# A plain first layer in block 1, x of block 2 transposed on PE, and another order of m-tiles in a chunk-attention and MLP kernel

## Chip, cores, metric

The kernel runs on one core of a Trainium2 chip. The metric is the device time of one execution in microseconds (us). A ratio is the mean time of one kernel's fast runs over that of the other's fast runs of the same rounds, so not quite the ratio of the medians quoted beside it. "Trace" below is one profiled execution; its span is 1.5 to 2 us less than the time measured for it. PE is the TensorE, DVE the VectorE, ACT the ScalarE, POOL the GpSimd; PSUM is the memory, in banks, that PE writes its products to. In the 40 slices of a profile's page, slices are counted from 0.

## The reference, cut

```python
def _attn_ref(q, k, v):                      # each (8, 8, 576, 64)
    # nine chunks of 64 per sequence; softmax attention inside each chunk
    scores = scale * np.matmul(q_c, k_c.transpose(0, 1, 2, 4, 3))
    ...
    return out.reshape(B, H, S, D)

def _moe_ref(x, w_in, w_out, beta):          # x (4608, 512), w_in (512, 2048), w_out (2048, 512)
    h = x @ w_in
    g = h * (1.0 / (1.0 + np.exp(-beta * h)))
    return (g @ w_out).astype(np.float32)
```

x is the attention's output, tokens by heads times head size. Inputs and output are float32; the kernel computes in float16 with float32 sums.

## The kernel before

The 4608 tokens are done in nine blocks of 512. Each block needs x transposed (`xt`, four tiles of 128 tokens), then L1 (16 m-tiles of 128 hidden features, Silu on ACT) and L2. From block 1 on, half of L1 (m-tiles 0 to 7) and all of L2 use seven half-size products in place of eight, after Strassen and Winograd; they need sums of x (`emit_xs`), of the weights (`emit_sw` for L1, `emit_tw` for L2) and of the hidden values (`emit_sum`). While block j is in its layers, scores (`emit_sc`) and value products (`emit_pv`) of block j+1 are slipped between its products. In the profile: L131 the DVE transposes of q and k (`T`), L159 a product of scores, L187 a value product, L202 and L204 its normalisation, L224 the copy of an x tile transposed on PE, L245 a plain m-tile, L278 to L281 `emit_xs`, L298 a product of a unit, L306, L319 and L333 the unit's snapshots and sums on DVE, L309 its Silu, L370 `emit_tw`, L356 to L362 `emit_sum`, L398 a product of L2. Of the tiles, `sc` holds scores, `hps` a plain m-tile, `wA` and `wX` a unit's products, and `oA` to `oD` those of L2, all in PSUM.

A transposed tile on PE, and one unit, which makes four m-tiles:

```python
    def emit_xp(i):
        xf = x16_t.pop(i)
        j, t0 = i // 4, (i % 4) * 128
        xps = ps_s.tile([128, KDM, 128], FP16, tag=f"sc{i % 2}", name="xps")
        for kk in range(KDM):
            nc.tensor.transpose(
                out=xps[:, kk, :], in_=xf[:, kk * 128:(kk + 1) * 128], identity=ident
            )
        nc.scalar.copy(out=xt_t[j][:, :, t0:t0 + 128], in_=xps)

    def unit(j, q, spacers):
        x = xt_t[j]
        ts = xs_t[j]
        up_, dn_ = slice(0, HT), slice(HT, BLK)
        b11, b21, b22 = x[:, 0:2, up_], x[:, 2:4, up_], x[:, 2:4, dn_]
        swr = [t.rearrange("p k (m i r) -> p k m r i", r=2, i=128) for t in sw]
        a11, a12, a22 = w_r[0][:, 0::2], w_r[0][:, 1::2], w_r[1][:, 1::2]
        bank = {"A": ps_s.tile([128, 2, HT], FP32, tag=f"sc{q}", name="wA")}
        xx = ps_x.tile([128, 2, 2, HT], FP32, tag="x", name="wX")
        bank["B"], bank["C"] = xx[:, 0], xx[:, 1]
        sb = {}

        def prod(b, a, rhs, first):
            for i in range(2):
                for kk in range(2):
                    nc.tensor.matmul(
                        out=bank[b][:, i, :], lhsT=a[:, kk, q, i, :], rhs=rhs[:, kk, :],
                        start=(first and i == 0 and kk == 0), stop=(kk == 1),
                        skip_group_check=True,
                    )

        def snap(nm, b):
            sb[nm] = u_p.tile([128, 2, HT], FP32, tag=nm, name=nm)
            nc.vector.tensor_copy(out=sb[nm], in_=bank[b])

        def silu(m, cols, src):
            nc.scalar.activation(
                out=gt_t[j][:, m, cols], in_=src, func=ACTF.Silu,
                scale=beta2[:, m % 2, m // 2:m // 2 + 1],
            )

        m1, m2 = 2 * q, 4 + 2 * q
        c1 = c_p.tile([128, 2, BLK], FP32, tag="c1", name="c1")
        prod("A", a11, b11, True)
        snap("u1", "A")
        prod("B", a12, b21, True)
        nc.vector.tensor_tensor(out=c1[:, :, up_], in0=bank["B"], in1=sb["u1"], op=ALU.add)
        spacers[0]()
        prod("A", swr[1], ts[1], False)
        snap("u2", "A")
        prod("C", swr[0], ts[0], True)
        snap("w1", "C")
        spacers[1]()
        prod("A", swr[2], ts[2], False)
        snap("u3", "A")
        sb["t"] = u_p.tile([128, 2, HT], FP32, tag="t", name="t")
        nc.gpsimd.tensor_tensor(out=sb["t"], in0=sb["u3"], in1=sb["w1"], op=ALU.add)
        spacers[2]()
        prod("A", a22, ts[3], False)
        prod("C", swr[3], b22, False)
        nc.vector.tensor_tensor(out=c1[:, :, dn_], in0=bank["C"], in1=sb["u2"], op=ALU.add)
        for i in range(2):
            silu(m2 + i, up_, bank["A"][:, i])
        for i in range(2):
            silu(m1 + i, slice(0, BLK), c1[:, i])
        for i in range(2):
            silu(m2 + i, dn_, sb["t"][:, i])
```

The first layer, plain and with units; a hook is other work slipped in ahead of an m-tile:

```python
    def L1_plain(j, hooks, nh):
        for m in range(nh):
            emit_h(j, m, 0, HT)
            hooks.get(-1 - m, lambda: None)()
        for m in range(nh):
            emit_h(j, m, HT, BLK)
            emit_g(j, m)
        for m in range(nh, KFF):
            emit_m(j, m)

    def L1(j, hooks={}, first=None):
        gt_t[j] = gt_p.tile([128, KFF, BLK], FP16, tag="gt", name="gt")

        def sp(m):
            def f():
                hooks.get(m, lambda: None)()
                emit_m(j, m)
            return f

        if first:
            first()
        unit(j, 0, [sp(8), sp(9), sp(10)])
        sp(11)()
        unit(j, 1, [sp(12), sp(13), sp(14)])
        for p in (0, 2):
            emit_sum(j, 3, p)
        sp(15)()
        for p in (0, 2, 1, 3):
            fill.extend([lambda w=w, p=p: emit_sum(j, w, p) for w in (1, 2)])
        hooks.get(KFF, lambda: None)()
```

The end of block 0's stretch on DVE, and the loop over blocks:

```python
        emit_sw()
        scale_w_out(0)
        scale_w_out(1)
        T1 = T_items(1)
        T1[0]()
        T1[1]()
        scale_w_out(2)
        T1[2]()
        T1[3]()
        scale_w_out(3)
        load_v(2)
        load_qk(3)
        emit_tw(1)
        emit_tw(2)
        ...
        emit_xp(7)
        emit_xs(1)
        emit_tw(4)
        emit_tw(3)
        for j in range(1, NB):
            na = j + 1
            if j == 1:
                order = (2, 2, 2, 2)
            elif j == 2:
                order = (3, 3, 4, 4)
            else:
                order = (j + 2,) * 4
            hooks = {m: (lambda b=b: T(b)) for m, b in zip((10, 11, 14, 15), order)}
            late = j <= 2
            if late:
                hooks[KFF] = lambda: [table(ACTF.Exp), emit_sc(2 * na)]
            L1(j, hooks)

            def pv(n):
                if na < NB:
                    emit_pv(4 * na + n)

            def sc(n):
                if na + 1 < NB and j > 1:
                    emit_sc(2 * na + 2 + n)

            if j > 1 and j + 3 < B or j == 1:
                load_qk(j + 3)
            mm, cB, cD, cC = steps_L2(j, last=(j == NB - 1))
            mm[0]()
            emit_sum(j, 3, 1)
            emit_sum(j, 3, 3)
            if not late:
                pv(0)
            dve(4)
            mm[1]()
            if late:
                pv(0)
                emit_sc(2 * na + 1)
            else:
                pv(1)
            cB()
            dve(2)
            mm[2]()
            pv(1 if late else 2)
            dve(2)
            mm[3]()
            pv(2 if late else 3)
            if not late:
                table(ACTF.Exp)
                sc(0)
            for p in range(4):
                emit_sum(j, 4, p)
            if j == 2:
                T(4, 2)
            mm[4]()
            cD()
            if late:
                pv(3)
                sc(0)
            mm[5]()
            if j < NB - 1:
                cC()
            if not late:
                sc(1)
            if j == 1:
                T(3, 2)
            if na < NB:
                emit_xs(na)
            mm[6]()
            if late:
                sc(1)
            table(ACTF.Silu)
            if j + 2 < B:
                load_v(j + 2)
```

The softmax here doesn't subtract the row's maximum and nothing guards it: scores larger than these inputs give would overflow.

## Time and profile before

| | before |
|---|---|
| time, median (runs) | 310.49 us (4 runs, 309.58 to 311.74) |
| span of the trace | 309.8 us |
| PE, DVE, ACT, POOL busy | 89, 73, 54, 33% |
| mean granted PE clock | 0.977 |
| block 0's L2 ends, block 1's L1 starts | 55.5 us |
| blocks 1, 2, 3, 4 (start of L1 to start of the next) | 36.5, 36.3, 33.3, 31.4 us |
| blocks 5, 6, 7, 8 | 29.5, 29.1, 28.2, 29.9 us |

PE's idle time is not spread out. Blocks 6 and 7 run at the pace that PE allows; blocks 1 and 2 are seven to eight microseconds longer for the same layers. A change that is to pay has to make the first blocks look like the last.

### The profile page before, as it was taken

To read this page: it belongs to the slowest core of one execution; us is meant where nothing else is said; L and a number is where in the kernel's file an instruction comes from. 1 tells how busy PE (TensorE), PEld (TensorE's weight loads), DVE (VectorE), ACT (ScalarE), POOL (GpSimd) and SP (SyncE) were. 2 spreads that over 40 slices of the span, in tenths; PEclk is the share of its full clock that TensorE was granted. 3 is DMA by queue.
4 is the path that set the end of the run, shared out by engine and by line. 5 is a ranking of instruction groups with operands and counts; after the bars stand their busy time and mean duration, and the time that the engine had idled before them with its cause. 6 is when DMAs were issued, how large, how long until landed. Compare 5 with 4: busy or idle time off the path is not lost.

```text
span 309.8 us, 8218 instructions
## 1 busy us (share of the span) xinstructions
PE 276.0 (89%) x3520; PEld 190.4 (61%) x3520; DVE 225.1 (73%) x415; ACT 168.8 (54%) x291; POOL 101.7 (33%) x110
## 2 busy tenths in 40 slices
PE   2689997498996999799989997999999999999995
PEld 0364443255883668555866586658866876676584
DVE  2682466768797879788868886889765976687584
ACT  1258333437713793557437733773577457536852
POOL 8632260014215161526107520741164111413300
PEclk9999997869997999999999999999999999999999
DMA  6999999900899039590949096903390330052003
GB/s 112 178 207 211 194 202 196 224 3 1 140 152 145 3 62 181 129 69 0 177 118 144 1 175 119 142 3 78 79 130 2 93 115 0 19 103 88 2 34 102
DMA packets 69588, 31.99 MB, mean 103 GB/s; under 512 B 53680, under 2 KB 63920, under 8 KB 69552
## 3 DMA queue, kind: packets, MB, share of 16 engines
q0 software_dynamic: 44960, 18.35, 48.7%
q1 hardware_dynamic: 24448, 12.99, 17.8%
q8 instruction: 27, 0.44, 0.6%
q10 hardware_dynamic: 144, 0.13, 0.1%
q14 instruction: 9, 0.07, 0.1%
HBM read 36.71 MB, written 9.44 MB: 149 GB/s over the span
## 4 chain that ended last, share of the span: by engine, by line
PE 45%; DVE 24%; DMA 19%; ACT 6%; issue 5%; POOL 1%; DVEq 0%; ACTq 0%; POOLq 0%
PE oA L398 11%; PE hps L245 11%; DMA w_out<-in_moe_w_out_dram 10%; PE wA L298 6%; DMA xt<-x 6%; PE wX L298 5%; DVE qT L131 4%; ACT gt L309 3%; PE oB L398 3%; DVE kT L131 3%; DVE c L333 3%; PE oC L398 3%; DMA vb<-in_v_dram 3%; DVE s L362 2%; PE oD L398 2%
## 5 line engine op out<-in xcount | busy, mean ns | idle before, releaser
L245 PE MATMUL hps<-xt,wi 128*128 128x512 f16 (+1 forms) x336 | 83.0, 378 | 1.4 <-ACT xt L224 1.3
L255 ACT ACTIVATE gt<-hps,beta 128x512 f16<-128x512 f32 x80 | 53.0, 680 | 36.7 <-PE hps L245 36.6
L398 PEld LDWEIGHTS <-s 128*128 128x128 f16 x496 | 46.3, 98 | 10.6 <-DVE s L362 4.7
L245 PEld LDWEIGHTS <-wi 128*128 128x128 f16 x336 | 33.4, 100 | 25.9 <-issue 4.1
L306 DVE COPY u<-wA 128x512 f32<-128x512 f32 x48 | 33.0, 688 | 17.5 <-PE wA L298 17.5
L329 POOL TENSOR_TENSOR t<-u,w 128x512 f32<-128x512 f32 x16 | 20.5, 1282 | 76.9 <-DVE u L306 76.9
L398 PE MATMUL oA<-tw,s 128*128 128x256 f16 x368 | 44.1, 273 | 0.0
L398 PEld LDWEIGHTS <-gt 128*128 128x128 f16 x384 | 35.8, 98 | 12.2 <-ACT gt L309 6.5
L298 PEld LDWEIGHTS <-sw 128*128 128x128 f16 x256 | 25.8, 101 | 21.3 <-issue 12.3
L409 ACT COPY u<-oA 128x512 f32<-128x512 f32 x24 | 14.1, 586 | 36.7 <-PE oA L398 36.1
L168 ACT ACTIVATE et<-sc 128x512 f16<-128x512 f32 x34 | 18.4, 593 | 28.1 <-PE sc L159 28.1
L99 POOL DMA_DIRECT2D vb<-in_v_dram x32 | 27.4, 876 | 10.1 <-DMA wi<-in_moe_w_in_dram 6.3
L204 DVE TENSOR_TENSOR x<-x,rd 128x512 f16<-128x512 f32 x34 | 23.5, 692 | 5.1 <-DMA xt<-x 4.0
L467 POOL TENSOR_TENSOR o<-t,o 128x512 f32<-128x512 f32 x7 | 8.9, 1271 | 55.5 <-ACT o L464 55.5
L298 PE MATMUL wA<-xs,sw 128*128 128x256 f16 x128 | 20.5, 286 | 6.9 <-DVE u L306 6.9
L298 PEld LDWEIGHTS <-wi 128*128 128x128 f16 x192 | 18.7, 98 | 9.4 <-issue 3.8
L131 DVE STREAM_TRANSPOSE qT<-qu 128x576 f32<-128x576 f32 x16 | 20.0, 1250 | 5.9 <-DMA qu<-in_q_dram 5.9
L635 ACT ACT_TABLE_LOAD x17 | 21.8, 1283 | 4.1 <-DVE oe L478 3.8
L309 ACT ACTIVATE gt<-c,beta 128x512 f16<-128x512 f32 x32 | 21.4, 715 | 4.0 <-DVE c L333 4.0
L131 DVE STREAM_TRANSPOSE kT<-ku 128x576 f32<-128x576 f32 x16 | 20.0, 1248 | 2.3 <-DMA ku<-in_k_dram 2.3
L436 POOL TENSOR_TENSOR w<-u,u 128x512 f32<-128x512 f32 x7 | 8.8, 1262 | 38.0 <-ACT u L409 38.0
L398 PE MATMUL oA<-w_out,gt 128*128 128x256 f16 x128 | 17.6, 274 | 3.4 <-ACT gt L309 3.4
(85 smaller groups left out, 405.3 us busy)
## 6 DMA issues: line engine op xcount, KB each, us to landing
out_dram<-osb SPq DMA_DIRECT2D x21, 256.0 KB, 2.3
vb<-in_v_dram POOLq DMA_DIRECT2D x32, 144.0 KB, 5.3
qu<-in_q_dram POOLq DMA_DIRECT2D x7, 576.0 KB, 7.8
ku<-in_k_dram POOLq DMA_DIRECT2D x7, 576.0 KB, 10.0
out_dram<-o SPq DMA_DIRECT2D x14, 256.0 KB, 2.2
wi<-in_moe_w_in_dram POOLq DMA_DIRECT2D x4, 512.0 KB, 12.4
w_out<-in_moe_w_out_dram POOLq DMA_DIRECT2D x4, 512.0 KB, 17.0
qu<-in_q_dram POOLq DMA_DIRECT2D x2, 288.0 KB, 5.5
```

The costliest lines, as they stand in the source:

```text
L99: nc.gpsimd.dma_start(out=t[64 * hp:64 * hp + 64, 2 * z:2 * z + 2, :, 0:D].rearrange("p s c d -> p (s c) d"), in_=v[b, h0:h0 + 2].rearrang ...
L131: nc.vector.transpose(out=dst[b][:, z].rearrange("p t r e -> p (t r e)").bitcast(FP32).rearrange("p (t r) -> p r t", r=RUN), in_=src[b][:, ...
L168: nc.scalar.activation(out=et, in_=sc[s], func=ACTF.Exp, scale=scale)
L204: nc.vector.tensor_tensor(out=yy, in0=src, in1=rr.to_broadcast(shape), op=ALU.mult,)
L245: nc.tensor.matmul(out=hps_t[j, m][:, c0:c1], lhsT=w_r[m // 4][:, 2 * z + e, m // 2 % 2, m % 2, :], rhs=xt_t[j][:, n, c0:c1], start=(n == ...
L255: nc.scalar.activation(out=gt_t[j][:, m, :], in_=hps, func=ACTF.Silu, scale=beta2[:, m % 2, m // 2:m // 2 + 1],)
L298: nc.tensor.matmul(out=bank[b][:, i, :], lhsT=a[:, kk, q, i, :], rhs=rhs[:, kk, :], start=(first and i == 0 and kk == 0), stop=(kk == 1), ...
L306: nc.vector.tensor_copy(out=sb[nm], in_=bank[b])
L309: nc.scalar.activation(out=gt_t[j][:, m, cols], in_=src, func=ACTF.Silu, scale=beta2[:, m % 2, m // 2:m // 2 + 1],)
L329: nc.gpsimd.tensor_tensor(out=sb["t"], in0=sb["u3"], in1=sb["w1"], op=ALU.add)
L398: nc.tensor.matmul(out=bank[name][:, i, :], lhsT=a[:, kk, i * 128:(i + 1) * 128], rhs=b[:, kk, :], start=(first and i == 0 and n == 0), st ...
L635: nc.scalar.activation(out=warm2, in_=warm, func=func, scale=1.0)
```

## The change

The intent: give DVE room where PE waits for it. Block 1's L1 becomes plain, which needs no x sums and no snapshots, so that L2's weight sums and the transposes of batches 2 and 3 fit beside it. Block 2's x goes through PE in place of the DMA transposes, so that block 2 can start with its sums ready and take the pattern of later blocks. In blocks 2 to 8 both units stand back to back in their m-tiles' order and two plain m-tiles follow the last unit, to cover its Silu. The diff, with nothing cut but context:

```diff
--- before.py
+++ after.py
@@ -236,7 +236,7 @@
-        if m == 0 and c0 == 0:
+        if m == 0 and c0 == 0 and j == 0:
@@ -525,6 +525,8 @@
+        if j:
+            gt_t[j] = gt_p.tile([128, KFF, BLK], FP16, tag="gt", name="gt")
@@ -532,7 +534,15 @@
+            hooks.get(m, lambda: None)()
+            if j and m == 8:
+                for p in (0, 2):
+                    emit_sum(j, 3, p)
+        if j:
+            for p in range(4):
+                fill.extend([lambda w=w, p=p: emit_sum(j, w, p) for w in (1, 2)])
+            hooks.get(KFF, lambda: None)()
@@ -546,10 +556,10 @@
-        sp(11)()
-        unit(j, 1, [sp(12), sp(13), sp(14)])
+        unit(j, 1, [sp(11), sp(12), sp(13)])
+        sp(14)()
@@ -609,6 +619,7 @@
+        emit_tw(1)
@@ -618,8 +629,6 @@
-        emit_tw(1)
-        emit_tw(2)
@@ -642,30 +651,25 @@
-        emit_xp(7)
-        emit_xs(1)
-        emit_tw(4)
-        emit_tw(3)
-            if j == 1:
-                order = (2, 2, 2, 2)
-            elif j == 2:
-                order = (3, 3, 4, 4)
+            late = j == 1
+            if late:
+                L1_plain(1, {
+                    -1: lambda: emit_xp(7), 3: lambda: emit_tw(3), 4: lambda: T(2), 5: lambda: T(2),
+                    6: lambda: emit_tw(2), 7: lambda: T(2), 9: lambda: T(2),
+                    10: lambda: emit_tw(4), 14: lambda: T(3), 15: lambda: T(3),
+                    KFF: lambda: [table(ACTF.Exp), emit_sc(4)],
+                }, 2)
-                order = (j + 2,) * 4
-            hooks = {m: (lambda b=b: T(b)) for m, b in zip((10, 11, 14, 15), order)}
-            late = j <= 2
-            if late:
-                hooks[KFF] = lambda: [table(ACTF.Exp), emit_sc(2 * na)]
-            L1(j, hooks)
+                L1(j, {m: lambda: T(j + 2) for m in (10, 13, 14, 15)})
-                    emit_pv(4 * na + n)
+                    emit_pv(4 * na + n, xbar=not late)
-                if na + 1 < NB and j > 1:
+                if na + 1 < NB:
@@ -680,40 +684,42 @@
-                emit_sc(2 * na + 1)
+                emit_sc(5)
+            if late:
+                emit_xp(8)
-            if not late:
+            if late:
+                emit_xp(9)
+            else:
-            if j == 2:
-                T(4, 2)
+            if late:
+                T(3, 2)
+                emit_xp(10)
-            if not late:
-                sc(1)
-            if j == 1:
-                T(3, 2)
+            if late:
+                emit_xp(11)
+            sc(1)
-            if late:
-                sc(1)
```

## The prediction

> **What bounds the kernel now.** I read the page first, then the waits of the TensorE, then the timeline stage by stage. One execution works through nine blocks of 512 tokens. In each, L1 (x by w_in, with Silu) is followed by L2 (by w_out). In blocks 1 to 8 both are wholly or half done with seven products in place of eight.
>
> ```profile
> span 309.8 us, 8218 instructions
> PE 276.0 (89%) x3520; PEld 190.4 (61%) x3520; DVE 225.1 (73%) x415; ACT 168.8 (54%) x291; POOL 101.7 (33%) x110
> ...
> PE   2689997498996999799989997999999999999995
> ...
> PEclk9999997869997999999999999999999999999999
> ```
>
> PE is the bound, but not everywhere: slices 6 to 8 (46 to 70 us) and 11 to 13 (85 to 108 us) have holes, and the granted clock falls in the same places. The rest is nearly full. The waits of the TensorE name the holes (us in total, times, longest):
>
> ```profile
> PE wA L298 <- DVE u L306: 6.9, 3, 3.4
> ...
> PE oA L398 <- ACT gt L309: 3.4, 12, 0.3
> PE oC L398 <- DVE s L362: 3.1, 5, 1.3
> PE x L187 <- DVE x L204: 2.2, 1, 2.2
> PE wX L298 <- DVE c L319: 1.7, 7, 0.6
> ```
>
> The first and fourth are the starts of blocks 1, 2 and 3 and the tail of block 0. The timeline at the end of block 0's L2 (start, length, engine):
>
> ```profile
> 46.17 1.21 DVE L370 TENSOR_TENSOR tw<-w_out 128x2048 f16<-128x2048 f16 x1
> ...
> 47.41 1.23 DVE L370 TENSOR_TENSOR tw<-w_out,tw 128x2048 f16<-128x2048 f16 x1
> ...
> 48.55 0.20 DVE L202 RECIPROCAL rd<-x 128x8 f32<-128x8 f32 x1
> ...
> 49.53 0.32 PE L187 MATMUL x<-vb,et 64*64 64x65 f16 x16 [2.17 <-DVE x L204]
> ```
>
> Two weight differences for L2 stand on the DVE ahead of the normalisation that PE needs, so PE idles 2.17 us. Ten us later the same again, at block 1's first unit:
>
> ```profile
> 58.70 1.22 DVE L370 TENSOR_TENSOR tw<-w_out,tw 128x2048 f16<-128x2048 f16 x1
> ...
> 59.84 1.22 DVE L370 TENSOR_TENSOR tw<-w_out 128x2048 f16<-128x2048 f16 x1
> 60.97 0.68 DVE L306 COPY u<-wA 128x512 f32<-128x512 f32 x1
> 61.71 1.01 PE L298 MATMUL wA<-xs,sw 128*128 128x256 f16 x4 [3.44 <-DVE u L306]
> ...
> 63.37 1.91 PE L245 MATMUL hps<-xt,wi 128*128 128x512 f16 x4
> ```
>
> PE idles 3.44 us and then runs at half clock: four 512-column matmuls show 1.91 us there and 1.03 later. Cut into half-microsecond windows, the granted clock is 0.50 from 49.7 to 53.1, until 66.7, and from 97.7 to 101.0 us. Each stretch follows a gap of over 2 us, none follows a gap of 1.2 us or less.
>
> **What the Trainium skill says.** "TensorE: Matmul & The Clock Gate", Part 1: the gate halves the clock after an idle window of about 3.4 us and lifts it after a busy one. The half and the 3.4 us lengths agree, but gaps of 2.2 us were enough here. The same page, "Back-to-back issue gap": N/2.4 + 2.5 ns, 216 ns for 512 columns. The trace agrees: an m-tile (four of them) advances PE by 0.865 us (228.30 to 229.16). The same page, Part 4: a transpose on PE lands in PSUM and needs a copy out, at 275 to 390 ns each. Here four together advance PE by only 0.24 us (54.18 to 54.42), and the copy on ACT takes 0.58. "ScalarE: Activation LUTs", "What ACT_TABLE_LOAD costs": 1283 ns; the trace has 1.28 us for each of 17.
>
> **The change, part by part,** as PE time between stage starts.
>
> *Tail of block 0.* tw1 moves to 31.9 us, where the DVE idles 1.49 us before its transposes; tw2 goes behind into block 1. The reciprocal then follows the last w_out scaling (ends 46.24) and not 48.55. PE no longer waits 2.17 us, nor runs 3.3 us at half clock. Walking units 13 to 15 through with 0.865 us per m-tile-sized group, 0.25 per PV and 0.24 per transposed tile, and one new wait of 0.4 us for the next normalisation, block 1's first matmul starts at 51.8 and not 55.5: -3.7.
>
> *L1 of block 1.* The eight m-tiles of the two units cost 8 x 0.865 = 6.9 us plain, where the 14 products took 14 x 0.435 = 6.1 (222.57 to 223.00 is one): 0.8 more. The change takes away the first-unit wait (3.44), the one before it (0.67), the second unit's and half the 4.9 us at half clock. Now 16 x 0.865 = 13.8, plus 0.25 for the last transposed tile, plus about 0.9 waiting for that tile's copy (ACT must first load its table, 1.28 + 0.2, then copy 0.58): 15.0 against 20.5 (55.5 to 76.0): -5.5. The DVE has tw3, tw2, tw4 (1.22 each) and six transposes (1.25 each) there, 11.2 us in 14, and nothing on PE waits for them before the scores at the end.
>
> *L2 of block 1.* It takes two score groups that block 2's L1/L2 used to hold (2 x 0.64) and four transposed tiles (4 x 0.25). The tiles share PSUM banks with the scores, so the scores behind tiles 10 and 11 must wait for ACT's copies, some 0.9 and 0.85 us; tile 11 itself waits 0.75 for the DVE, which has two transposes ahead of it. The old 0.6 wait for kT goes. 16.0 becomes 19.3: +3.3.
>
> *Block 2.* It starts with its x sums ready: 2.26 us of wait, 0.4 more, and 1.6 us of half clock go, and it takes the pattern of block 4 before (31.4 us) in place of its own 36.3. With what the unit order changes there (-0.5, below) it is 30.9: -5.4.
>
> *Block 3.* Its start loses the waits 0.91, 1.21 and 0.56 that the late scores and the late DMA transposes caused: 33.3 becomes 30.9: -2.4.
>
> *Order of m-tiles, blocks 2 to 8.* Two things trade:
>
> ```profile
> 228.50 0.69 DVE L333 TENSOR_TENSOR c<-wX,u 128x512 f32<-128x512 f32 x1 [1.13 <-PE wX L298]
> ```
> ```profile
> 235.75 0.60 PE L398 MATMUL oA<-w_out,gt 128*128 128x256 f16 x4
> 236.59 0.28 PE L398 MATMUL oA<-w_out,gt 128*128 128x256 f16 x1 [0.24 <-ACT gt L309]
> 237.20 1.37 PE L398 MATMUL oA<-w_out,gt 128*128 128x256 f16 x11 [0.33 <-ACT gt L309]
> ```
>
> Sixteen matmuls of L2's first product advance PE by 2.76 us (235.75 to 238.51) where other products take 1.75: 1.0 us is lost to the last unit's Silu, more than the 0.57 that the bracketed waits add up to. A second m-tile (0.865) behind the unit hides nearly all of it, -0.95. But unit 1 now follows unit 0 directly. Its product B needs the bank that L333 reads until 229.19; PE would be there at 228.74: +0.5. Net -0.5. With transposes on the DVE (blocks 2 to 5) a 0.36 us wait in unit 1 goes too, -0.9 for L1. Blocks 2 to 4 give 0.4 back at the one place where they wait for DMA:
>
> ```profile
> 155.84 0.69 DVE L204 TENSOR_TENSOR x<-x,rd 128x512 f16<-128x512 f32 x1 [1.87 <-DMA xt<-x]
> ...
> 156.92 0.39 PE L398 MATMUL oC<-w_out,s 128*128 128x256 f16 x2 [1.04 <-DVE s L362]
> ```
>
> The q/k load is issued at the end of L1 and holds the DMA engines for about 9 us, so the transposes land at a fixed time after L1's end however early L2 gets there. So block 4 gets -0.5, block 5 -0.6 (DVE a little behind), blocks 6, 7, 8 -0.5 each.
>
> Sum: -3.7 - 5.5 + 3.3 - 5.4 - 2.4 - 0.5 - 0.6 - 1.5 = -16.3 us. 311.06 - 16.3 = 294.8. I add 0.7 for an even chance that the three waits in block 1's L2 (2.5 us in 6) halve the clock once (1.6): 295.5.
>
> **Rivals.** *New waits eat the gain.* PE transposes sit in L2 of block 1 next to scores on the same two banks. If ACT runs late there or the clock halves, 2 to 4 us go: 298. For it: three serial hand-offs PE, ACT, PE. Against: in 128 to 132 us PE waited 2.7 us in pieces without losing its clock. *Loads become the bound.* Block 1 now needs q, k and v of batches 2 and 3 some 4 to 13 us sooner, and DMA is at 9 tenths until 62 us. q/k of batch 3 are issued at 43.0 and 45.4 and take about 15 us, so they land near 61, when their transposes come. If not, the scores wait: 300. *The unit order loses.* If unit 1's wait is 1 us and not 0.5, seven blocks lose 0.5 each: 299. *More is won:* waits of block 1's L2 overlap with late matmul ends, or blocks 2 to 4 have no DMA wait: 291.
>
> **Range and chances.** The gains at 47 to 66 and 92 to 101 us (about 11 us) rest on waits that the code plainly removes; the rest on estimates. Repeats spread by 2 us. So 291.5 to 300. Faster by over 2% needs under 304.8, and would fail only if half the sum did.
>
> **What would show it.** Right: no DVE wait at 47 us; granted clock without a dip before 70 us; L1 of block 1 about 15 us; block 2 about 31 us; L2's first product at 1.75 us in blocks 2 to 8; waits of wX on L333 of about 0.5 us in each. Wrong: a dip of clock in block 1's L2, that L2 over 21 us, waits of the DVE on q/k loads in block 1, or block 2 above 33 us.

## The result

| | before | after |
|---|---|---|
| time, median (runs) | 310.49 us (309.58 to 311.74) | 295.15 us (4 runs, 294.66 to 296.39) |
| ratio, 95% interval | | 0.951 (0.946 to 0.956) |
| span of the trace | 309.8 us | 294.6 us |
| mean granted PE clock | 0.977 | 0.994 |

The first lines of the page, and the busy tenths in 40 slices, after:

```profile
span 294.6 us, 8175 instructions
## 1 busy us (share of the span) xinstructions
PE 271.5 (92%) x3520; PEld 188.7 (64%) x3520; DVE 212.2 (72%) x399; ACT 170.3 (58%) x291; POOL 99.4 (34%) x108
...
PE   2689999999899998999899979999999999999995
...
PEclk9999999999979999999999999999999999999999
```

The holes of PE at 46 to 70 us and 85 to 108 us have closed, and of three stretches at half clock one is left, in slice 11. The waits of the TensorE, after (us in total, times, longest):

```profile
PE oC L398 <- DVE s L362: 4.3, 7, 1.5
PE wX L298 <- DVE c L333: 2.4, 7, 0.3
...
PE sc L159 <- ACT xt L224: 1.2, 2, 0.7
...
PE x L187 <- DVE x L204: 0.2, 1, 0.2
```

Gone are the 6.9 us of wA on L306 and the 3.4 of oA on the Silu; the 2.2 of L187 on the normalisation fell to 0.2. New are 2.4 us of wX on L333, seven times (0.34 or 0.35 each), and 1.2 us of scores on the copies of x tiles. One old wait grew: oC on the sums, from 3.1 to 4.3.

By stages of PE, from the two traces (L2 of block 1 counted from its first scores):

| stage | before, us | predicted | after, us |
|---|---|---|---|
| start of block 1's L1 | at 55.5 | at 51.8 | at 51.2 |
| L1 of block 1 | 20.5 | 15.0 | 15.0 |
| L2 of block 1 | 16.0 | 19.3 | 21.1 |
| block 2 | 36.3 | 30.9 | 30.7 |
| block 3 | 33.3 | 30.9 | 30.5 |
| block 4 | 31.4 | 30.9 | 30.9 |
| block 5 | 29.5 | 28.9 | 28.8 |
| block 6 | 29.1 | 28.6 | 28.8 |
| block 7 | 28.2 | 27.7 | 27.8 |
| block 8 and the end | 29.9 | 29.4 | 29.8 |

The trace after is of the slowest of the four executions, 296.39 us at a mean clock of 0.994, which is what one stretch of 3.4 us at half clock gives. The other three ran at 0.998 to 1.0 in 294.66 to 295.29 us, so the median is that of executions without the stretch. Where no dip comes (three traces below), L2 of block 1 takes 19.65 us counted as in this table, and not 21.1.

Three places in the timeline after. At the end of block 0 and the start of block 1 the normalisation and the value product follow without a wait, and the plain layer runs 64 matmuls in one piece after 0.69 us for the last tile's copy:

```profile
45.55 0.19 DVE L202 RECIPROCAL rd<-x 128x8 f32<-128x8 f32 x1
...
46.74 0.32 PE L187 MATMUL x<-vb,et 64*64 64x65 f16 x16
...
53.17 13.12 PE L245 MATMUL hps<-xt,wi 128*128 128x256 f16 x64 [0.69 <-ACT xt L224]
```

L2 of block 1 is the stage that came out longer than predicted:

```profile
79.18 0.64 PE L159 MATMUL sc<-qT,kT 32*64 32x64 f16 x56 [0.67 <-ACT xt L224]
...
80.48 0.26 PE L159 MATMUL sc<-qT,kT 32*64 32x64 f16 x8 [0.66 <-DVE kT L131]
...
80.67 3.17 PE L398 MATMUL oC<-w_out,s 128*128 128x256 f16 x16
...
84.94 0.70 PE L159 MATMUL sc<-qT,kT 32*64 32x64 f16 x63 [0.49 <-ACT xt L224]
```

Two waits on the copies of x tiles stand where they were expected. The one on kT was not: these scores reach into batch 3, whose last transposes stand in this very stage. After them the product takes 3.17 us where 1.92 is usual, because the clock has halved. In windows of one microsecond (busy us of PE, granted clock, DMA share, GB/s):

```profile
80.00:81.00 1.00, 0.52 (x11) 1.00 0.05 16
81.00:82.00 1.00, 1.00 (x8) 0.58 0.10 36
82.00:83.00 1.00, 1.00 (x7) 0.50 0.66 226
```

A block without DMA waits, block 6, shows the trade of the m-tile order:

```profile
214.93 0.60 PE L298 MATMUL wX<-xt,wi 128*128 128x256 f16 x4 [0.35 <-DVE c L333]
...
221.94 1.97 PE L398 MATMUL oA<-w_out,gt 128*128 128x256 f16 x16
223.83 0.32 PE L187 MATMUL x<-vb,et 64*64 64x65 f16 x16
```

L2's first product now advances PE by 1.89 us (221.94 to 223.83) where it was 2.76, and unit 1's product B starts 0.95 us after A (213.98 to 214.93) where a product takes 0.44: 0.87 won, 0.5 lost. In block 2, the DMA wait is as it was in blocks 3 and 4 before:

```profile
112.26 0.69 DVE L204 TENSOR_TENSOR x<-x,rd 128x512 f16<-128x512 f32 x1 [2.13 <-DMA xt<-x]
```
```profile
113.34 0.39 PE L398 MATMUL oC<-w_out,s 128*128 128x256 f16 x2 [0.55 <-DVE s L362]
```

### The profile page after: what moved, and what is told of

Its sections match the earlier page's. It is cut to its first block, busy times and chain, and to the rows that moved or that the text cites. A ratio compares the mean times of both kernels' runs of the same rounds, so it can differ in the third digit from the quotient of the medians.

```text
span 294.6 us, 8175 instructions
## 1 busy us (share of the span) xinstructions
PE 271.5 (92%) x3520; PEld 188.7 (64%) x3520; DVE 212.2 (72%) x399; ACT 170.3 (58%) x291; POOL 99.4 (34%) x108
## 4 chain that ended last, share of the span: by engine, by line
PE 62%; DMA 18%; DVE 12%; issue 3%; POOL 2%; ACT 2%; ACTq 0%; DVEq 0%; POOLq 0%
PE hps L245 20%; PE oA L398 14%; DMA xt<-x 8%; DMA w_out<-in_moe_w_out_dram 7%; PE wA L298 7%; PE wX L298 6%; PE oC L398 5%; PE oB L398 4%; DMA wi<-in_moe_w_in_dram 3%; PE sc L159 3%; DVE qT L131 2%; DVE s L362 2%; PE oD L398 2%; DVE c L333 2%; PE ops L497 2%
## 5 line engine op out<-in xcount | busy, mean ns | idle before, releaser
L245 PE MATMUL hps<-xt,wi 128*128 128x512 f16 (+1 forms) x376 | 85.3, 365 | 1.4 <-ACT xt L224 1.3
L255 ACT ACTIVATE gt<-hps,beta 128x512 f16<-128x512 f32 x88 | 58.5, 681 | 22.7 <-PE hps L245 22.7
L245 PEld LDWEIGHTS <-wi 128*128 128x128 f16 x376 | 36.7, 98 | 30.4 <-issue 1.9
L306 DVE COPY u<-wA 128x512 f32<-128x512 f32 x42 | 29.0, 690 | 17.2 <-PE wA L298 17.2
L329 POOL TENSOR_TENSOR t<-u,w 128x512 f32<-128x512 f32 x14 | 18.1, 1292 | 37.6 <-DVE u L306 37.6
L298 PEld LDWEIGHTS <-sw 128*128 128x128 f16 x224 | 21.9, 98 | 8.5
L298 PEld LDWEIGHTS <-wi 128*128 128x128 f16 x168 | 16.4, 98 | 9.6 <-issue 6.4
L360 POOL TENSOR_TENSOR s<-gt 128x512 f16<-128x512 f16 x16 | 18.2, 1156 | 11.8 <-ACT gt L255 11.8
L159 PE MATMUL sc<-qT,kT 32*64 32x64 f16 x1088 | 13.5, 195 | 9.1 <-DVE kT L131 6.7
L309 ACT ACTIVATE gt<-c,beta 128x512 f16<-128x512 f32 x28 | 18.7, 714 | 3.7 <-DVE c L333 3.7
```

What stands on the lines that cost most here:

```text
L159: nc.tensor.matmul(out=sc[a % 2][o0:o0 + 64, z, c, :], lhsT=kk[:, cb * CH:(cb + 1) * CH, e], rhs=qq[:, cb * CH:(cb + 1) * CH, e], start=(e ...
L245: nc.tensor.matmul(out=hps_t[j, m][:, c0:c1], lhsT=w_r[m // 4][:, 2 * z + e, m // 2 % 2, m % 2, :], rhs=xt_t[j][:, n, c0:c1], start=(n == ...
L255: nc.scalar.activation(out=gt_t[j][:, m, :], in_=hps, func=ACTF.Silu, scale=beta2[:, m % 2, m // 2:m // 2 + 1],)
L298: nc.tensor.matmul(out=bank[b][:, i, :], lhsT=a[:, kk, q, i, :], rhs=rhs[:, kk, :], start=(first and i == 0 and kk == 0), stop=(kk == 1), ...
L309: nc.scalar.activation(out=gt_t[j][:, m, cols], in_=src, func=ACTF.Silu, scale=beta2[:, m % 2, m // 2:m // 2 + 1],)
```

## The experiments

The question is which parts carried the 15 us, whether by the waits that the prediction named, and where the rest of block 1 and the DMA waits come from. Theory: the prediction's own sum. Rivals: that the weight sums' move alone did it; that the order of the m-tiles only swaps waits; that PE transposes were needed because DMA transposes come late. All outputs are right. One call's kernels ran on one chip with the kernel before beside them. There its median was 309.7 us in the first call, 310.95 in the second and 311.3 in the third, so ratios are compared across calls, and times only within one.

**Old order of the m-tiles, the rest as changed.**

```diff
-        unit(j, 1, [sp(11), sp(12), sp(13)])
+        sp(11)()
+        unit(j, 1, [sp(12), sp(13), sp(14)])
         (sums)
-        sp(14)()
         sp(15)()
-   hooks at (10, 13, 14, 15)
+   hooks at (10, 11, 14, 15)
```

> The changed kernel with only the order of the m-tiles in blocks 2 to 8 put back (one m-tile between the units, one behind). My theory: the last unit's Silu again costs L2's first product about 1.0 us in each of seven blocks, the 0.5 us wait of unit 1 on L333 goes, and blocks 2 to 4 hide part of it behind their DMA wait: about 3 us longer than the changed kernel, 298 us, ratio to before 0.96; first product about 2.7 us instead of 1.9, no wait of wX on L333. Rival 1: the reorder only swaps one wait for another and is worth nothing: 295, ratio 0.951. Rival 2: every block gains its whole 0.95: 301.5.

Measured: 299.48 us, ratio 0.966 (0.962 to 0.970) against 0.951. That is 1.5% of 310 us, 4.6 us. In the traces, where one has a clock dip in block 1 and the other has none, blocks 2 to 8 alone differ by 4.2 us (211.5 against 207.3 us from block 2's L1 to the end): 0.8, 0.8, 0.7 and 0.75 in blocks 2 to 5, about 0.4 in blocks 6 to 8. The waits of oA on the Silu are back, those of wX on L333 are gone:

```profile
PE oA L398 <- ACT gt L309: 4.0, 14, 0.3
```

So the order is worth more than the 3 us expected: the blocks with a DMA wait gave less of it back than I had reckoned.

**The weight sums put back into block 0's tail.**

```diff
-        emit_tw(1)          # ahead of T1
         (T1, scale_w_out, loads)
+        emit_tw(1)
+        emit_tw(2)
-   6: lambda: emit_tw(2),   # hook of block 1
```

> The changed kernel with L2's first two weight differences put back at the end of block 0's chain on DVE, ahead of the normalisation that PE waits for. Theory: PE waits about 2.2 us near 47 us and then runs some 3.4 us at half clock, so the first matmul of block 1 comes 3.7 us later and the rest follows: 299 us, ratio 0.963. Rival: the delay is caught up in block 1's plain layer or at the q/k loads, since DVE has slack there: within 1 us of the changed kernel.

Measured: 297.16 us, ratio 0.960 (0.954 to 0.967), about 3 us longer than the changed kernel by the ratios. The wait is there, the dip that should follow it is not:

```profile
49.12 0.32 PE L187 MATMUL x<-vb,et 64*64 64x65 f16 x16 [2.06 <-DVE x L204]
```

Window from 50 to 51 us of this run:

```profile
50.00:51.00 1.00, 1.00 (x23) 1.00 2.28 145
```

The same microsecond of the kernel before, which had waited 2.17 us at the same place:

```profile
50.00:51.00 1.00, 1.00 (x6) 0.50 2.35 161
```

The delay is not caught up: block 1's L1 starts at 53.6 us and takes the same time. So the move of the sums is worth its wait, 2 us and some, in every execution. The half clock that the prediction counted with it, 3.3 us long, did not come in this trace. One of the other three executions took 299.96 us at a mean clock of 0.988, the rest 296.66 to 297.32 at 0.998 to 1.0; so half clock comes in some executions and not in others.

**Block 1's L1 with units again, the sums and transposes spread over its m-tiles.**

```diff
-   L1_plain(1, {...})
+   emit_xp(7); emit_xs(1)
+   L1(1, {10: T(2), 12: emit_tw(3), 13: T(2),
+          14: [T(2), emit_tw(2)], 15: [T(2), emit_tw(4)],
+          KFF: [table(Exp), emit_sc(4)]})
+   T(3, 2) behind the layer sums of L2
```

> The changed kernel with block 1's first layer done with seven products again; weight differences and transposes spread over its spacers, two transposes of batch 3 moved into L2. Theory: PE saves 0.8 us of products but waits for the x sums (1.0 to 1.6 us), for DVE snapshots behind differences and transposes, and L2 of block 1 waits for late sums: 2 to 5 us longer than the changed kernel, 297 to 300 us. Rival: moving the differences out of the tail was all that counted and plain was not needed: 0.8 us shorter, 294.4.

Measured: 303.36 us, ratio 0.978 (0.973 to 0.982): more than 8 us longer than the changed kernel. From L1's start to L2's first product block 1 takes 22.0 us, as it did before the change (21.9), though no weight sum stands in its way at the start:

```profile
55.65 0.61 PE L298 MATMUL wA<-xs,sw 128*128 128x256 f16 x4 [1.17 <-DVE u L306]
...
67.44 0.60 PE L298 MATMUL wA<-xs,wi 128*128 128x256 f16 x4 [0.51 <-DVE u L306]
...
73.37 0.43 PE L159 MATMUL sc<-qT,kT 32*64 32x64 f16 x16 [2.66 <-DVE kT L131]
```

The wait has moved from the start to the end, because DVE has twelve snapshots and sums of the units and four x sums more to do, and the transposes come out last. There is half clock in it too, from 56.1 and from 73.2 us (slices 7 and 9). This is one placement of several possible; it shows that moving the sums out of the tail is not enough, not that no placement with units could do better.

**Block 2's x by DMA again.**

```diff
-   emit_pv(4 * na + n, xbar=not late)
+   emit_pv(4 * na + n, xbar=True)
-   emit_xp(8) ... emit_xp(11)
```

> The changed kernel with block 2's x transposed by DMA again and no transposes on PE in L2 of block 1. Theory: in the changed kernel the q/k load there ends by 66 us and the DMA engines stand idle until 80, so the DMA transposes would land within 3 us and PE saves four transposed tiles (1.0 us) and two waits on ACT copies (0.67 and 0.49); the wait on kT (batch 3) stays and grows. L2 of block 1 falls from 21.1 to about 19.2: 2 us shorter, 293 us. Rival: the DMA transposes come late as they did before the change, and L1 of block 2 waits for its x sums: 1 to 2 us longer, 297.

Measured: 295.49 us, ratio 0.953 (0.950 to 0.956): the same as the changed kernel. Neither side had it right. The two waits on copies are gone, and the DMA transposes land in time for PE (block 2's first unit waits for nothing), but ahead of the scores that need batch 3's kT PE gains nothing, for it runs into the wait for kT, now three times as long:

```profile
81.32 0.25 PE L159 MATMUL sc<-qT,kT 32*64 32x64 f16 x8 [2.17 <-DVE kT L131]
```

Both traces get past kT 29.3 us after the start of block 1's L1. So up to there the transposes of batch 3 set the pace, and what stands beside them is hidden. Behind it the last transposed tile and the wait on its copy do go: L2 of block 1 takes 19.5 us from its first product against 20.5, with half clock of 3.4 us in both traces. That 0.9 us does not show in the span, because block 0 happened to end later here (block 1's L1 starts at 52.06 us against 51.23), and the times of four executions do not resolve it.

**The changed kernel again, as control.** No edit.

> The changed kernel as it is, as the control of this call: 294.5 to 295.5 us, ratio to before 0.951. If its trace shows another place of the half-clock stretch, or none, in an otherwise equal schedule, then the dips depend on where the clock's windows happen to lie, not on the kernel alone; without a dip the span should be about 1.4 us shorter, 293.2.

Measured: 295.6 us, ratio 0.951 (0.948 to 0.955). The trace has the dip in the same slice as before, so the two profiled executions agreed. The other executions did not: three of the six ran at a mean clock of 1.0 (294.69 to 295.63 us), which leaves no room for a dip, and the profiled one at 0.994 took 296.39. With the four of the result, ten executions of this kernel are on record, three of them at 0.994 or below and seven at 0.997 to 1.0. So the same program can have the dip or not.

**Batch 3's transposes all in block 1's L1.**

```diff
-   14: lambda: T(3), 15: lambda: T(3),
+   14: lambda: T(3, 2), 15: lambda: T(3, 2),
-   T(3, 2)                  # in L2 of block 1
```

> The changed kernel with all four transposes of batch 3 in block 1's L1, none in its L2. Theory: the first score group of L2 of block 1 no longer waits 0.66 us for kT, x of tile 11 is ready when PE wants it, the two waits on ACT copies (0.67 and 0.49) stay: L2 of block 1 from 19.0 without a clock dip to about 18.2, 0.8 us less in time, 294 us; up to 2 less if the dip there goes with the wait. Rival: DVE has no room in L1 (the q/k load of batch 3 lands at 62.6) and the layer sums come late: L2's first or third product waits and nothing is won.

Measured: 294.28 us (294.16 for the five fast executions), ratio of the fast runs 0.948 (0.945 to 0.951), about 1.1 us under the control by the ratios, near the 0.8 expected; its fast executions (293.86 to 294.66) all lie below those of the control (294.69 to 296.39). One of six executions, the profiled one, took 398.28 us at a granted clock of 0.65 from about 12 us to its end. Nothing but that clock is read from its trace here; the trace with the load moved as well (below) shows the effect on L2.

**The q/k load of blocks 2 to 4 ahead of L1.**

```diff
     late = j == 1
+    if j > 1 and j + 3 < B:
+        load_qk(j + 3)
     (L1)
-    if j > 1 and j + 3 < B or j == 1:
-        load_qk(j + 3)
+    if j == 1:
+        load_qk(4)
```

> The changed kernel with the q/k load of blocks 2 to 4 issued before their L1 instead of behind it. Theory: that load is what holds the DMA engines while the transposes of x wait; moved away, the waits of oC on s (0.7 to 1.5, with a second of 0.28) go, and blocks 2, 3, 4 (30.7, 30.5, 30.9 us) take the length of block 5, 28.8: 5.5 us less, 289.5, ratio 0.933. Rival: three x buffers and the transposes' own time make the wait, or the v load and stores stand in the way as much: less than 1.5 us won, 293 or more.

Measured: 289.64 us, ratio 0.933 (0.931 to 0.936), as expected. Blocks 2, 3 and 4 all take 28.8 us. The waits of oC on the sums, 4.3 us before this edit, are now:

```profile
PE oC L398 <- DVE s L362: 0.2, 1, 0.2
```

This shows the cause that the prediction had only argued. In the changed kernel the load is issued at 102.0 and 102.7 us, and x of the first tile, put to the DMA at 104.29, lets its buffer go only at 112.26. The four transposes of that block land 4.9 to 7.9 us after their issue. Without the load in the way they land after 2.4 to 4.5 us, and the buffer is free in time.

**All three: early load, early transposes of batch 3, x by DMA.** The edits of those three runs, together.

> Batch 3's transposes early, block 2's x by DMA and the q/k load early, together. Theory: in the run with DMA transposes alone the saved PE time came back as a 2.17 us wait for kT; with kT early L2 of block 1 falls to about 16.5 us (20.5 in the changed kernel's trace), and with the 5.5 us of blocks 2 to 4: 285.5 us, ratio 0.92. Rival: DMA transposes in block 1 land too late for the x sums once PE is earlier, and L1 of block 2 waits 1 to 2 us: 287.5; or PE transposes never mattered: 289.

Measured: 288.79 us (287.36 to 291.54), ratio 0.931 (0.927 to 0.936), some 3 us longer than expected; span of the trace 285.7. With kT early, L2 of block 1 does fall, to 15.7 us from its first product (20.5 in the changed kernel). But the first rival holds too: the x sums of block 2 wait for the last DMA transpose, and L1 of block 2 takes 15.6 us and not 13.7:

```profile
82.60 0.42 DVE L278 TENSOR_TENSOR xs<-xt 128x512 f16<-128x512 f16 x1 [1.57 <-DMA xt<-x]
...
85.87 0.60 PE L298 MATMUL wA<-xs,sw 128*128 128x256 f16 x4 [1.42 <-DVE u L306]
```

So PE transposes may serve a purpose for the last tile; the last run tests that.

**The new order alone in the kernel before.** The edit is the first experiment's, the other way round.

> The kernel before with nothing but the new order of the m-tiles (in its blocks 1 to 8). Theory, from the run that took the order out of the changed kernel: blocks 3, 4, 5 gain about 0.75 us each, blocks 6, 7, 8 about 0.37, blocks 1 and 2 nothing or a little, since scores stand between their layers and cover the Silu: 3.3 us less, 307.5, ratio 0.989. Rival: the gain needs the rest of the change: under 1.5 us, ratio over 0.995.

Measured: 306.63 us, ratio 0.986 (0.981 to 0.991). From block 3's L1 to the end of the trace it takes 178.4 us where the kernel before takes 181.5, and its waits of oA on the Silu are gone. Its trace also happens to lack the half clock at 50 us, behind a wait of 2.0 us, which makes its span shorter than the order alone does. The order's worth of 3 us and more thus stands with and without the rest of the change.

**Early load and early transposes of batch 3, PE transposes kept.** Two of the edits above, together.

> Early load and batch 3's transposes early, with the PE transposes kept. Theory: against the run with the early load alone the kT wait (0.66) and the wait for tile 11's x go, L2 of block 1 from 19.0 to about 18.1: 288.7 us, ratio 0.930, trace about 287. The rival: DVE has no room in L1 of block 1 and nothing is won: 289.6.

Measured: 288.31 us, ratio 0.927 (0.923 to 0.931). L2 of block 1 takes 18.2 us from its first product, against 19.0 with the early load alone: 0.85, where 0.9 was expected. Two waits on copies of x tiles (1.2 us) stay.

**As the run with all three, but the last x tile through PE.**

```diff
-   emit_pv(4 * na + n, xbar=not late)
+   emit_pv(4 * na + n, xbar=not (late and n == 3))
    (emit_xp(8), (9), (10) removed, emit_xp(11) kept; load and T(3) as above)
```

> As the run with early load, early transposes of batch 3 and x by DMA, but the last tile of block 2's x goes through PE, since its DMA transpose came about 3 us after its normalisation and cost L1 of block 2 a 1.4 us wait for the x sums. Theory: L2 of block 1 16.4 us (0.25 for the tile, 0.5 for the bank it shares with the scores, over 15.7), L1 of block 2 back from 15.6 to 13.7: trace 284.5, time 286.5, ratio 0.922. Rival: the x sums are late because DVE is, not because of the transpose: L1 of block 2 stays above 15 us and nothing is won, 288.8.

Measured: 286.89 us (286.35 to 287.15), ratio 0.922 (0.919 to 0.926): the fastest kernel, some 3% under the changed one (0.922 against 0.951). L2 of block 1 takes 16.6 us, L1 of block 2 is back at 13.7, and one wait of the kind is left there:

```profile
81.65 0.70 PE L159 MATMUL sc<-qT,kT 32*64 32x64 f16 x63 [0.53 <-ACT xt L224]
```

## Why the prediction was right

*The sum.* It said 295.5 us within 291.5 to 300; 295.15 was measured. Most stages came within 0.4 us of their own line, so the sum is in the main not the luck of errors that cancel. Two stages are further off and cancel in part, and some luck is in the last half microsecond: the forecast holds 0.7 us for a dip of the clock that the median execution does not have, and it starts from one execution of 311.06 us where the median was 310.49. (Its remark on the 2% is loose: from 311.06 to 304.8 is 6.2 of the 16.3 us, so some three fifths of the sum would have had to fail, not half.)

*Tail of block 0* (-3.7): -4.3 in the trace. The wait of 2.17 us is gone as argued. 0.6 of it is chance: in that execution the last part of w_out landed earlier, and its scaling began at 44.32 and not 44.93 us. In the traces that share this part of the program, block 1's L1 starts anywhere from 50.8 to 52.1 us. The half clock counted with it belongs to an execution, not to the kernel: with the wait put back it did not come in the trace.

*L1 of block 1* (-5.5): 15.0 us as predicted, to the tenth. With units put back, in the one placement tried, it is as long as before, though no weight sum stands at its start; plain is what gave DVE the time.

*L2 of block 1* (+3.3): +5.1 in the trace with the dip, +3.7 in those without. This is the weakest stage of the prediction. Its own terms do not add up to its total: 2 x 0.64 + 4 x 0.25 + 0.9 + 0.85 + 0.75 - 0.6 is +4.2. The transposed tiles, the two waits on their copies and their sizes (0.9 and 0.85 expected; 0.67 and 0.49 shown in brackets, 0.83 and 0.82 as PE advances without a dip) were seen rightly. The 0.75 us that tile 11 was to wait for DVE did not appear. In its place came a wait of 0.66 us that I had not seen: the first late scores need the last transposes of batch 3. So +3.7 against +3.3 is luck in part. The clock dip, entered at an even chance with 0.7 us, came whole in the profiled execution (from the first product L2 takes 20.5 us with it, 19.0 in the traces without), and by the mean clocks in three of ten.

*The signs of being wrong.* Three of the four that the prediction named came, each small: the dip of clock in L2 of block 1, that L2 at 21.1 us and so over 21, both in the profiled execution, and one wait of DVE for the k load of batch 3 in L1 of block 1, 0.69 us at 62.60 us, for which PE did not wait there (that load took 17.8 us, where about 15 had been reckoned). The dip cost 1.5 us, where the rival of new waits had named 2 to 4 in all.

*Blocks 2 and 3* (-5.4, -2.4): -5.6 and -2.8. They start with their sums ready and show no wait before the first unit. The PE transposes are not what did this: with block 2's x by DMA again, block 2 also takes 30.7 us. Which of the other moves did it is not separated by a run.

*Order of the m-tiles*: per block right in kind, a little small in size. Taken out or put in alone it is worth 3 to 4.6 us. I had let blocks 2 to 4 give back 0.4 us each at their DMA wait, so that they would gain 0.5; they gain 0.7 to 0.8. In blocks 6 to 8, where I had 0.5 each, it is 0.4.

*The load as cause of the DMA wait*: argued in the prediction, shown by moving the load.

*The rule of the clock* given there, a dip after gaps of over 2 us and none after gaps of 1.2 us or less, did not hold. In its own trace the second stretch begins at 60.0 us, inside the gap that ends at 61.71, and not after it. There was no dip after a gap of 2.06 us; there was one after gaps of 0.67 and 1.17 us (units put back, from 56.1 us), and one after two gaps of 0.67 and 0.66 us within two microseconds, while the same two gaps passed without a dip in three other traces (old order, sums in the tail, load early). What decides it in an execution stays open.

## What to carry to other kernels

Where one engine waits for another at a few places, ask what else that other engine is made to do just ahead of each, and whether a costlier form on the waiting engine (plain products here, 0.8 us dearer) frees it: that stage fell by 5.5 us, with the weight sums moved as well. When taking work away changes nothing, look for the wait that ends at the same moment; here much of the x tiles' saved time came back as a longer wait for kT. Early kT alone took 0.8 us off L2 of block 1, and together with the removed tiles 3.3 (19.0 to 15.7). And look at bulk loads before small transfers that the chain needs: issuing one load a layer earlier was worth more than a third of the whole change.

## What the Trainium skill lacked or had wrong

- "TensorE: Matmul & The Clock Gate", Part 1, speaks of an idle window of about 3.4 us before the clock halves, and gives no length for shorter gaps that can halve it too. Here it halved after single gaps of 2.2 and 2.3 us and after two of 0.67 and 0.66 us close together; it did not after one of 2.06 us, nor after the same two in three other traces. Its remark that windows run free and that the outcome varies from run to run agrees with that. Each stretch of half clock before the last microseconds lasted 3.4 us, or twice that (6.8 us from 60.0 us in the kernel before, and from 58.2 us with the order alone).
- The same page, Part 4, gives 275 to 390 ns for a transpose on PE. The trace has 219 ns for one, its end modelled, and in a row four advanced PE by 0.24 us; what cost more was the copy of 0.58 us and the bank behind it, waits of 0.5 to 0.7 us.
- The same page, Part 1, has as clock states half, full, 13/16 under the load of three cores of a die, and a warning of a monitor stuck at a quarter. One of six executions of one kernel, a program on one core, ran at 0.65 from about 12 us to its end and took 398.28 us and not 294. No page has that.
- "DMA: Bandwidth & Descriptors", "Issuing engines are not separate DMA queues", says that transfers from several engines share the DMA engines and interleave, and gives no figure for a short one behind a bulk load. Here a buffer that a DMA transpose of one x tile read came free 8.0 us after its issue behind a load of 1152 KB; the four transposes of that block landed 4.9 to 7.9 us after their issue, and 2.4 to 4.5 us with the load moved, which was worth 5.6 us by the ratios.
